# Eight weight combinations moved from a mix of GpSimd and VectorE to VectorE alone, in a fused sliding-window attention and feed-forward kernel

## The chip, the cores and the metric

The kernel runs on one core of one Trainium2 chip. A core has a matrix engine (TensorE, "PE" in the profile; its weight loads are "PEld"), a vector engine (VectorE, "DVE"), an activation engine (ScalarE, "ACT"), a general engine (GpSimd, "POOL") and a synchronization engine (SyncE, "SP") that here only issues transfers. The metric is the device time of one execution in microseconds (us). Before the change it is 304.42 us, the median of three runs (302.83, 304.42 and 305.78).

## What is computed

Attention over 8 batches, 8 heads, 576 positions, 64 numbers per head. Each position attends to the positions at most 32 away:

```
scores = q @ k.T / sqrt(64);  mask = |pos_i - pos_j| <= 32
attn   = softmax(where(mask, scores, -1e9))
x      = (attn @ v), heads side by side          # 4608 tokens x 512
h      = x @ w_in                                # 512 -> 2048
g      = 0.5 * h * (1 + tanh(c * (h + 0.044715 h^3)))
out    = g @ w_out                               # 2048 -> 512
```

## The kernel before

**Tiles.** The 4608 tokens are cut into nine tiles of 512 (`t` = 0 to 8). While tile `t` goes through the feed-forward part, the attention of batch `b = t + 1` is computed in its gaps, as far as there is one. Attention writes the transposed result into `xT`; `ffn_in` (L563) multiplies it with `w_in`, ScalarE applies the gelu (L571), and `ffn_out` (L737) multiplies with `w_out`.

**Fewer products.** The second matrix product of tiles 1 to 8 is done by a scheme of the Strassen-Winograd kind: seven products of half-size blocks in place of eight, after sums of blocks have been made. The sums of gelu's output are made at L680 by VectorE for every tile. In the last two tiles (7 and 8) part of the first product is done in that way too (`in_mixed`, L615). This needs combinations of blocks of `w_in`: for each of two units, A and B, four of them, S1 = A21 + A22, S2 = S1 - A11, S3 = A11 - A21 and S4 = A12 - S2. They are made once, by `in_w` (L590), each one an instruction on 128 x 512 numbers of type fp16, and are kept in SBUF. S2 reads S1, and S4 reads S2; S3 reads `w_in` alone.

**Order.** It is written by hand. Each engine executes its own instructions in the order of the program. The main loop counts steps `i` = 0 to 112 in each tile; a step issues one matmul of `ffn_out`, and a plan says at which step a piece of attention is issued: scores (`s`, L454), the multiplication of the exponentials by the mask (`m`, L476), the sums and the weighting by v (`v`, L481 and L491), and the normalizing of a group (`x`, L526, or L532 for a batch's tail). The second group's normalizing, `x1`, stands at step 50; the tail's mask, `m4`, stands at step 84. Behind each product of `ffn_out` VectorE takes the result out of PSUM or adds it up (L748, L750, L752, L757, L760, L766, L775).

**GpSimd's queue.** Near the start of each tile, GpSimd waits for a transfer (the copy `after`, L952) and issues five loads of v for the next batch (L194 four times, then L198). Its next work in tiles 3 and 4 is the pair of combinations for unit B; then come the tile's stores (L699, L697), which wait for the last sums of the tile. GpSimd doesn't take part in the steps: a combination that is issued at step 92 runs on it as soon as the queue ahead is empty and its inputs are there.

Of the kernel before, what the change touches and what calls it, by code (L numbers as in the profile page):

```python
# [78 lines left out]
def kernel(  # L79
# [9 lines left out]
    nc = tc.nc  # L89
    B, H, S, D = q.shape  # L90
# [4 lines left out]
    NT = NTOK // 512  # L95
# [473 lines left out]
    def gelu(t, n):  # L569
        fc = column(t, n)  # L570
        nc.scalar.activation(gTs[t][:, fc, :], phs[fc], AF.Gelu_apprx_tanh)  # L571
        if t and n % 4 == 3:
            sums(t, n // 4)
# [3 lines left out]
    def in_w(eng, unit, *which):  # L577

        i = UNITS[unit]
        A11, A12, A21, A22 = (w_in16[:, d:d + 2, c + 256 * i:c + 256 * i + 256] for c in (0, 1024) for d in (0, 2))  # L580
        if (unit, "s") not in mixed:
            halves = [(rawp if unit == "A" else yp).tile([128, 2, 2, 256], FP16, name="wc" + unit + str(x),
                                                         tag=("qr", "kr")[x] if unit == "A" else "yo") for x in range(2)]
            mixed[unit, "s"] = [half[:, x] for half in halves for x in range(2)]
        S1, S2, S3, S4 = mixed[unit, "s"]
        mixed[unit, "w"] = dict(A11=A11, A12=A12, A22=A22, S1=S1, S2=S2, S3=S3, S4=S4)
        for x in which:
            dst, a, b, op = ((S1, A21, A22, ALU.add), (S2, S1, A11, ALU.subtract),
                             (S3, A11, A21, ALU.subtract), (S4, A12, S2, ALU.subtract))[x - 1]
            eng.tensor_tensor(dst, a, b, op=op)  # L590
# [77 lines left out]
    def combine(i, eng):  # L668
        dst, x, y = wino["todo"][i]
        eng.tensor_tensor(dst, x, y, op=ALU.subtract)  # L670
# [240 lines left out]
    for t in range(NT):  # L911
        b = t + 1
        att = b < B
        if t:
            for fc in range(begun):
                ffn_in(t, fc, 3, 4, then=False)
            for fc in range(begun):
                gelu(t, fc)
            if att and b > 1:
                parts = cast_and_turn(b)  # L920
            if t >= NT - 2:
                if t == NT - 2:
                    in_x(t)
                in_mixed(t)
            for fc in range(begun, NF if t < NT - 2 else 0):
                ffn_in(t, fc)
                if t == 1 and fc == 3:
                    parts[0]()
                    combine(4, nc.vector)
                if t == 1 and 6 <= fc < 10:  # L930
                    cast_v(2, fc - 6)
                if t == 1 and 9 <= fc < 14:
                    parts[1](fc - 9)
                if t == 1 and fc == 8:
                    trans_tails(1, psO.tile([128, 8, 128], FP16, name="pt", tag="O"))
                if t == 2 and fc == 10:
                    parts()
                if t > 1 and fc == 8 and att:
                    pair_v(b, nc.vector.tensor_copy)
        plan = PLAN_0 if not t else PLAN_1 if t == 1 else PLAN if att else {40: "v-1", 66: "x-1"} if t == B - 1 else {}  # L940

        def group(g):
            return (b, g) if g >= 0 else (b - 1, 4)

        if plan and t:
            load_table(exp_set)
        if t and b + 1 < B:
            load_qk(b + 1)
        ods = {}
        for i in range(113 if t else 65):  # L950
            if t and i == (4 if t > 1 else 46) and b + 1 < B:
                nc.gpsimd.tensor_copy(after, KLs[b % 2][:, 3, 0:1])  # L952
                load_v(b + 1)
                if t == 1:
                    load_tails(3, nc.gpsimd)
            for act in plan.get(i, "").split():
                kind, at = act[0], int(act[act.index("@") + 1:]) if "@" in act else None
                g = int(act[1:].split("@")[0])
                if kind == "w":
                    if g == 3:  # L960
                        cast_w(wo[g], w_out16[:, 12:16, :], cs=(0, 1), on_dve=(0,))
                    else:
                        cast_w(wo[g % 3], w_out16[:, 4 * (g % 3):4 * (g % 3) + 4, :], on_act=(1, 3),
                               cs={1: range(4), 2: (0, 1), 5: (2, 3)}[g])
                elif kind == "e":
                    cast_vt(1) if g == 4 else cast_v(1, g)
                elif kind == "k":
                    cast_early(1, g, (nc.vector, nc.vector))
                    if g == 2:
                        cast_tails(0, nc.gpsimd, even)  # L970
                elif kind == "t":
                    trans_tails(0, spare(at)[0], even)
                elif kind == "r":
                    trans_pair(1, g, *spare(at), copy=nc.scalar.copy if g == 2 else nc.vector.tensor_copy)
                elif kind in "np":
                    pair = psS.tile([128, 2, 512], FP32, name="ps_od", tag=f"S{at}")
                    for x in range(2):
                        if kind == "n":
                            sum_up(1, g + x, pair[:, x, :], groups[(1, g + x)])
                        else:  # L980
                            ods[g + x] = (pair[:, x, :], lts[g + x])
                            times(1, g + x, pair[:, x, :], groups.pop((1, g + x)))
                    if kind == "n":
                        n = size(1, g)
                        lts[g], lts[g + 1] = lt4[:, g, :], lt4[:, g + 1, :]
                        for x in range(2):
                            nc.scalar.activation(lts[g + x][:, 0:n], pair[:, x, 0:n], AF.Ln)
                        for x in range(2):
                            nc.scalar.activation(lts[g + x][:, 0:n], lts[g + x][:, 0:n], AF.Exp, scale=-1.0)
                elif kind == "u":  # L990
                    cast_w(wo[g], w_out16[:, 12:16, :], on_act=(3,), cs=(2, 3))
                    cast_tails(1, nc.gpsimd)
                    load_qk(2)
                elif kind == "c":
                    if g == 1:
                        B12 = combine_w()
                    combine(g, nc.vector)
                elif kind == "s":
                    score(*group(g), at)
                    if t == 1 and g == 4:  # L1000
                        load_table(gelu_set)
                elif kind == "d":
                    pair_chunk(b, g, nc.vector.tensor_copy)
                elif kind == "m":
                    mask(*group(g))
                elif kind == "v":
                    bb, gg = group(g)
                    o, d = weigh(bb, gg, at)
                    ods[g] = (o, invert(bb, gg, d))
                    if t and g < 0 and b + 1 < B:  # L1010
                        load_vt(b + 1)
                    if t > 1 and g == (3 if att else -1):
                        load_table(gelu_set)
                else:
                    spread(*group(g), *ods[g])
            if t == NT - 2 and i == 84:
                in_x(t + 1)
            if t in (3, 4) and i == 92:
                in_w(nc.gpsimd, "B", *((1, 2) if t == 3 else (3, 4)))
            if t == NT - 3 and i in (86, 90):  # L1020
                in_w(*((nc.vector, "A", 1, 2) if i == 86 else (nc.gpsimd, "A", 3, 4)))
            if t == 2 and i in (40, 44):
                store(0, *later[1 if i == 40 else 3])
            if t == 1 and i == 30:
                cast_vt(2)
                store(0, *later[0])
                store(0, *later[2])
            if t == 1 and i in PAIR_1:
                pair_v(2, nc.vector.tensor_copy, PAIR_1[i])
            if t == 0 and i < 64:  # L1030
                ffn_out_0(*ORDER_0[i])
            elif t and i < 112:
                ffn_out(t, i)
        if t == 0:
            wino_rest(B12)
            load_table(gelu_set)
        else:
            ffn_last(t)
        begun = 3 if t < NT - 1 else 0
        for fc in range(begun):  # L1040
            ffn_in(t + 1, fc, 0, 3)
# [28 lines left out]
```

## Time and profile before

The page gives the profiled execution by its span alone; of the three times, the one that lies nearest to this span is 305.78 us.

| | |
|---|---|
| times of the three runs | 302.83, 304.42, 305.78 us |
| span of the profiled execution | 305.7 us |
| PE busy | 288.9 us (95%) |
| DVE busy | 214.1 us (70%) |
| ACT busy | 195.7 us (64%) |
| POOL busy | 99.7 us (33%) |
| mean granted TensorE clock | 0.992 |
| L590 on POOL | 6 instructions, 1.16 to 1.61 us each |
| L590 on DVE | 2 instructions, 0.42 us each |

A row of the timeline has the start in us, the duration in us, the engine, the line, the operation, what it writes and reads, its shape, and in brackets how long its engine was idle before it and what ended this. Rows that follow each other on one engine with the same line are merged, with their number behind an x. The rows of the chain of waits have start, duration and the engine or transfer that the end of the program can be traced back to. The rows of the window table have the window, its length, busy time and number of instructions for PE, PEld, DVE, ACT and POOL, then the granted TensorE clock as a share of full speed, the DMA share and GB/s.

### The profile page before, as it was taken

Reading aid. Unit: us, or ns where it says so; the run is one execution under the profiler, and the core shown is the slowest. Engines: PE = TensorE matmul, PEld = TensorE weight load, DVE = VectorE, ACT = ScalarE, POOL = GpSimd, SP = SyncE. Lnnn points to the kernel's source line nnn. Section 1 sums busy time; section 2 is a strip of 40 time slices with the busy share of each in tenths; the row PEclk is TensorE's granted clock in tenths of the full one; section 3 lists DMA queues with packets and bytes.
Section 4 is the critical chain, followed back from the end, with each engine's and each line's share of the span. In section 5 each row is a group of like instructions: output and inputs, shape, how many; then the busy total and the mean of one; then the engine's idle time right before and its main releaser. Section 6 shows DMA issues by size and latency. Waiting matters only on the chain.

```text
span 305.7 us, 7286 instructions
## 1 busy us (share of the span) xinstructions
PE 288.9 (95%) x2941; PEld 184.7 (60%) x2941; DVE 214.1 (70%) x467; ACT 195.7 (64%) x313; POOL 99.7 (33%) x149
## 2 busy tenths in 40 slices
PE   7879999899899899999999799999999999999994
PEld 2434444445674388448844586468646867786683
DVE  4562577789876866958685948866896678865672
ACT  5865767669576776579657844787578755725700
POOL 3425515301574070607180905141540060006000
PEclk9999999999999999999999989999999999999999
DMA  7999999999699999899987993989694022004013
GB/s 220 203 303 385 368 282 250 226 154 223 174 225 202 171 243 215 162 147 219 168 189 121 239 145 84 145 205 182 114 188 65 2 54 88 2 0 136 3 38 102
DMA packets 115944, 50.76 MB, mean 166 GB/s; under 512 B 97495, under 2 KB 109399, under 8 KB 115910
## 3 DMA queue, kind: packets, MB, share of 16 engines
q1 hardware_dynamic: 86756, 37.62, 58.7%
q0 software_dynamic: 28032, 11.62, 25.8%
q10 hardware_dynamic: 1122, 1.06, 1.1%
q8 instruction: 23, 0.38, 0.6%
q14 instruction: 11, 0.09, 0.1%
HBM read 36.70 MB, written 9.44 MB: 151 GB/s over the span
## 4 chain that ended last, share of the span: by engine, by line
PE 57%; DMA 20%; SPq 10%; ACT 6%; DVE 4%; issue 1%; POOL 0%; DVEq 0%
PE mm L737 26%; PE mm L563 11%; PE ph L563 10%; SPq L182 5%; DMA wst<-in_moe_w_in_dram 5%; DMA tr<-in_q_dram 3%; DMA kr<-in_k_dram 3%; DMA KT<-k 3%; DMA wst<-in_moe_w_out_dram 2%; PE ps_s L454 2%; SPq L240 2%; PE pu L615 2%; DVE s L680 2%; PE ps_d L481 2%; ACT gT L639 2%; DMA tr<-in_k_dram 2%
## 5 line engine op out<-in xcount | busy, mean ns | idle before, releaser
L563 PEld LDWEIGHTS <-w_in 128*128 128x128 f16 x512 | 49.6, 98 | 58.8 <-DVE w_in L228 1.0
L563 PE MATMUL ph<-xT,w_in 128*128 128x512 f16 x256 | 64.1, 379 | 1.2 <-DVE w_in L228 0.5
L563 PE MATMUL mm<-xT,w_in 128*128 128x512 f16 x256 | 63.9, 379 | 0.1
L571 ACT ACTIVATE gT<-mm 128x512 f16<-128x512 f32 x60 | 35.6, 597 | 33.3 <-PE mm L563 32.7
L737 PEld LDWEIGHTS <-s 128*128 128x128 f16 x512 | 49.4, 98 | 7.6 <-issue 0.9
L699 POOL DMA_DIRECT2D out_dram<-y x55 | 32.5, 599 | 60.1 <-DVE y L766 45.9
L737 PE MATMUL mm<-t,s 128*128 128x256 f16 x376 | 45.1, 273 | 0.6 <-DVE y L750 0.2
L737 PEld LDWEIGHTS <-gT 128*128 128x128 f16 x384 | 36.5, 99 | 8.0 <-issue 0.7
L467 ACT ACTIVATE pe<-ps_s 128x960 f16<-128x960 f32 (+1 forms) x31 | 29.6, 976 | 17.7 <-PE ps_s L454 17.5
L571 ACT ACTIVATE gT<-ph 128x512 f16<-128x512 f32 x58 | 32.2, 599 | 10.7 <-PE ph L563 10.7
L680 DVE TENSOR_TENSOR s<-gT 128x512 f16<-128x512 f16 x64 | 26.8, 419 | 15.0 <-ACT gT L571 14.0
L737 PE MATMUL mm<-w_out,gT 128*128 128x256 f16 x256 | 34.3, 280 | 0.1
L104 ACT ACT_TABLE_LOAD x18 | 23.1, 1283 | 2.2 <-issue 1.9
L516 ACT ACTIVATE lt<-ps_d 128x480 f32<-128x480 f32 (+2 forms) x28 | 15.6, 556 | 12.1 <-PE ps_d L481 8.4
L517 ACT ACTIVATE lt<-lt 128x480 f32<-128x480 f32 (+3 forms) x36 | 21.1, 586 | 1.1
L476 DVE TENSOR_TENSOR pe<-pe,band 128x960 f16<-128x960 f16 x28 | 21.0, 765 | 0.9 <-ACT pe L467 0.9
L491 PEld LDWEIGHTS <-V 128*64 128x64 f16 x520 | 14.1, 112 | 7.2 <-DVE V L204 2.8
L194 POOL DMA_DIRECT2D V<-in_v_dram x20 | 17.9, 910 | 1.1 <-issue 0.7
L737 PE MATMUL mm<-t,gT 128*128 128x256 f16 x128 | 16.3, 273 | 0.0
L680 DVE TENSOR_TENSOR s<-s,gT 128x512 f16<-128x512 f16 x32 | 15.3, 478 | 1.1
L454 PE MATMUL ps_s<-QT,KT 64*64 64x128 f16 (+3 forms) x576 | 13.5, 216 | 2.3 <-DMA KT<-k 1.5
L454 PEld LDWEIGHTS <-KT 64*64 64x64 f16 x576 | 9.9, 106 | 8.6 <-issue 3.8
(148 smaller groups left out, 398.4 us busy)
## 6 DMA issues: line engine op xcount, KB each, us to landing
kr<-in_k_dram SPq DMA_DIRECT2D x31, 256.0 KB, 10.9
qr<-in_q_dram SPq DMA_DIRECT2D x6, 1024.0 KB
wst<-in_moe_w_in_dram SPq DMA_DIRECT2D x7, 512.0 KB, 9.3
V<-in_v_dram POOLq DMA_DIRECT2D x20, 128.0 KB, 8.6
wst<-in_moe_w_out_dram SPq DMA_DIRECT2D x2, 1024.0 KB
wst<-in_moe_w_out_dram SPq DMA_DIRECT2D x4, 512.0 KB
qr<-in_q_dram SPq DMA_DIRECT2D x7, 256.0 KB, 8.6
out_dram<-y POOLq DMA_DIRECT2D x6, 192.0 KB, 5.9
```

Of the source, the lines that this page charges most:

```text
L104: nc.scalar.add_instruction(mybir.InstLoadActFuncSet(name=nc.get_next_instruction_name(), act_func_set_id=which, ins=[], outs=[]))
L194: nc.gpsimd.dma_start(V[:, c, :, :], v[b, :, 128 * c:128 * c + 128, :].rearrange("h p d -> p h d"))
L454: nc.tensor.matmul(sides[h][64 * half:64 * half + 64, 4 * n * r:4 * n * r + 4 * n].rearrange("k (j p) -> k j p", j=4)[:, :, p0 - q0:p1 - q ...
L467: nc.scalar.activation(pe, ps[:, :, 0:w], AF.Exp, scale=SCALE)
L476: nc.vector.tensor_tensor(pe, pe, m.rearrange("k (o j) p -> k o j p", o=1).broadcast_to(list(pe.shape)), op=ALU.mult)
L516: nc.scalar.activation(lt[:, 0:n], d[:, 0:n], AF.Ln)
L517: nc.scalar.activation(lt[:, 0:n], lt[:, 0:n], AF.Exp, scale=-1.0)
L563: nc.tensor.matmul(ph, w_in16[:, dc, fc * 128:fc * 128 + 128], xT[:, dc, t * 512 % RING:t * 512 % RING + 512], start=(dc == 0), stop=(dc = ...
L571: nc.scalar.activation(gTs[t][:, fc, :], phs[fc], AF.Gelu_apprx_tanh)
L680: nc.vector.tensor_tensor(dst, x, y, op=op)
L699: eng.dma_start(out_v[b, j, q0 + p:q0 + p + e, cols], yo[m:m + e, cols])
L737: nc.tensor.matmul(pys["apart"][:, 0:256] if apart else py[:, blk, :], lhsT, wino[w][:, f, :], start=(new and i % (8 if one else 16) == 0) ...
```

## The change

All eight combinations are made by VectorE. In tiles 3 and 4 the two of unit B are issued at step 52, behind the second group's normalizing, in place of step 92 on GpSimd. In tile 6 the first two of unit A are issued at step 52 too, in place of step 86, and the last two at step 86, behind the tail's mask, in place of step 90 on GpSimd. Nothing else differs: the instructions of PE, ACT and SP keep their order, VectorE has six more and GpSimd six fewer.

```diff
-            if t in (3, 4) and i == 92:
-                in_w(nc.gpsimd, "B", *((1, 2) if t == 3 else (3, 4)))
-            if t == NT - 3 and i in (86, 90):
-                in_w(*((nc.vector, "A", 1, 2) if i == 86 else (nc.gpsimd, "A", 3, 4)))
+            if t in (3, 4) and i == 52:
+                in_w(nc.vector, "B", *((1, 2) if t == 3 else (3, 4)))
+            if t == NT - 3 and i in (52, 86):
+                in_w(nc.vector, "A", *((1, 2) if i == 52 else (3, 4)))
```

## The prediction

> **What bounds the kernel now.** I read the busy times first: PE is busy for 288.9 of 305.7 us, so time is lost or won only where PE waits or runs slowly. Next I read the chain of waits, and in it the starts of the tiles' first matmuls of `ffn_in` (start, duration, what):
>
> ```profile
> 122.97 0.65 PE mm L563 x3
> ...
> 153.38 0.65 PE mm L563 x3
> ...
> 187.51 0.65 PE mm L563 x3
> ...
> 217.93 0.65 PE mm L563 x3
> ...
> 248.35 0.65 PE mm L563 x3
> ```
>
> These open tiles 3, 4, 5, 6 and 7. Their distances are 30.41, 34.13, 30.42 and 30.42 us. Three tiles agree to 0.01; tile 4 is 3.72 longer with the same work. This is what I have to explain, since one of the three places of the change lies in it. The timeline of DVE, POOL and PE there:
>
> ```profile
> 170.70 1.54 DVE L476 TENSOR_TENSOR pe<-pe,band 128x960 f16<-128x960 f16 x1
> ...
> 172.16 2.30 DVE L476 TENSOR_TENSOR pe<-pe,band 128x960 f16<-128x960 f16 x1
> ...
> 172.03 0.72 POOL L198 DMA_DIRECT2D V<-in_v_dram  x1
> 172.74 1.20 POOL L590 TENSOR_TENSOR wcB<-w_in 128x512 f16<-128x512 f16 x1
> 173.86 1.61 POOL L590 TENSOR_TENSOR wcB<-w_in,wcB 128x512 f16<-128x512 f16 x1
> ...
> 174.52 0.39 PE L481 MATMUL ps_d<-pe,ones 128*64 128x480 f16 x2 [1.60 <-DVE pe L476]
> ```
>
> The reader is to see two masks on VectorE, which take 0.65 each in tile 5 (1.22 for the merged two), here 1.54 and 2.30. The second one ends at 174.46. That is 0.52 after GpSimd's first combination ends (172.74 + 1.20 = 173.94), about one mask's own duration, and GpSimd's second combination is stretched to 1.61 from 1.16 in tile 3. So mask and combination took turns. PE waited 1.60 for this mask. The window table then shows the clock:
>
> ```profile
> 173.00:174.00 1.00, 0.00 (x0) 0.00 (x0) 1.00 (x1) 0.97 (x3) 1.00 (x2) 1.00 2.34 161
> 174.00:175.00 1.00, 0.41 (x4) 0.13 (x4) 1.00 (x3) 0.36 (x1) 1.00 (x1) 0.89 1.62 182
> 175.00:176.00 1.00, 1.00 (x17) 0.81 (x18) 1.00 (x2) 0.95 (x2) 0.47 (x1) 0.50 1.74 181
> ```
>
> Right behind the idle stretch the granted clock falls to 0.50, and it stays there through the window 177 to 178. PE's next 29 matmuls of L737 start at 175.53, against 142.74 + 30.41 = 173.15 if tile 4 had followed tile 3's rhythm: 2.38 are lost by waiting. The other 3.72 - 2.38 = 1.34 are lost at half clock: these 29 take 4.56 in the chain, 3.27 in tile 3.
>
> **What the change removes.** Six combinations leave GpSimd: 1.31 + 1.16 (tile 3), 1.20 + 1.61 (tile 4), 1.17 + 1.16 (tile 6), 7.61 us of an engine that is 33% busy. Its own time is worth nothing; what counts is whom these six held up.
>
> - Tile 3: the third mask took 1.16 in place of 0.65 beside L198 and the first combination. The tile lasted 30.41, so PE had cover for 0.51. Gain 0.
> - Tile 6: an L680 sum took 1.71 beside the first combination of A, against 0.42 for its kind. The tile lasted 30.42, so this too was covered: the product that reads these sums comes later. Gain 0. The tile's stores, now behind S4 at 247.91, can start when L766 ends at 247.33. Nothing waits for them, since the stores of tiles 7 and 8 end the program. Gain 0.
> - Tile 4: the case above. The first mask's extra 0.89 (1.54 - 0.65) was over before any combination ran, so the change doesn't remove it. The second mask then starts at 172.16 as before and, with no combination beside it, takes 0.65, to 172.81. L532 follows (0.56, it overlaps the mask's end by 0.08), to 173.29, and releases the bank for PE's L491 0.04 later, at 173.33. In tile 3's rhythm that is due at 142.42 + 30.41 = 172.83. So 0.50 of the 2.38 stays. PE idles about 0.4 in place of 1.6. Gaps of up to 1.53 elsewhere (PE idle until 107.06, for a transfer) passed with the clock at 1.00, so I take the 1.34 as gone. Gain 3.72 - 0.50 = 3.2.
>
> **What it adds.** Six instructions on VectorE, 0.88 for two (245.85 to 246.73, the pair it already makes in tile 6). At step 52 the pair stands between the second normalizing and L757, which waits for PE:
>
> ```profile
> 240.16 0.65 DVE L526 TENSOR_TENSOR xT<-ps_o,lt 128x480 f16<-128x480 f32 x1
> 242.47 0.69 DVE L757 TENSOR_TENSOR y<-mm,y 128x512 f32<-128x512 f32 x1 [1.66 <-PE mm L737]
> ...
> 245.85 0.42 DVE L590 TENSOR_TENSOR wcA<-w_in 128x512 f16<-128x512 f16 x1
> ```
>
> This idle stretch is 1.66 in tile 6, 1.66 in tile 3 (L757 at 147.51), and 1.59 in the disturbed tile 4 (181.57). It hides 0.88 with at least 0.71 to spare: cost 0. If the cover were gone, L757, the next mask and PE's sums behind it would come up to 0.88 late, per place. The second pair of tile 6 takes exactly the place that S1 and S2 have now, ahead of L766: cost 0. The new waits are S2 on S1, on the same engine (0.04 between the two rows at 245.85), and the buffers: the tiles that unit B takes over were free when GpSimd wrote them at 143.74, and the slot is at about 145.9. Unit A's buffers were free at 223.69; the slot is at 240.8. GpSimd doesn't read SBUF beside any of the slots: in tile 3 its v loads are issued by 143.76 and its next row is at 152.66. A combination beside nothing on GpSimd bounds the cost from below at 0; from above by 0.88 x 3 = 2.6 if all cover were lost.
>
> [...]
> [...]
>
> **The sum.** 305.7 - 3.2 + 0 = **302.5** in the profiled execution's own time, 305.7 by its span. The median of the three runs is 1.3 below that, 304.42, and the range of the three is 2.95, about the size of tile 4's loss: I read 302.83 as a run with little of the disturbance, and 304.42 as one with the wait but without the half clock (305.7 - 1.34 = 304.4). The three times alone don't prove that. So I take 302.5 for the median of after too, 0.6% below the median of before. A run of after with no loss in tile 4 gives 305.7 - 3.72 = 302.0.
>
> **Rivals.**
>
> 1. *GpSimd's transfer issues hold the masks, not the combinations.* The first mask of tile 4 was late before any combination had begun, beside L194 and L198; that speaks for it. Against it: in tile 5 two masks beside L194 took 1.22 together. Then mask 2 waits for L198 until 172.75 and ends at 173.40, L532 at 173.88, L491 starts at 173.92, 1.09 late. That is 302.0 + 1.1 = 303.1, or 304.4 if half clock follows.
> 2. *The disturbance is rare.* If the median run of before had little of it, there is nothing to win, and after stays at about 304.4. For it: the lateness starts with an excess of 0.89 that tiles 3 and 5 don't have. Against it: the spread of the three times.
> 3. *VectorE becomes late, and the time is slower than before.* The place is step 52 of tiles 3, 4 and 6. From the point where VectorE reaches it more than 0.71 late, L757 and the mask behind it are pushed; the price is up to 0.88 per place, and 1.34 if PE's wait then costs it the clock. One such place leaves 302.0 + 2.2 = 304.2; all three 302.0 + 6.7 = 308.7. For it: masks were up to 2.5 late in tile 4. Against it: PE was late with them, and the slot was still 1.59 wide.
> 4. *It doesn't do what it says.* The order of VectorE's program shows the eight combinations where the text puts them, so only their effect is open. I give this no chance of its own.
>
> **How the numbers follow.** Forecast (301.4 to 303.0): 0.60. Rival 1 (303.0 to 304.4): 0.16. Rival 2 (304.0 to 304.8): 0.10. Rival 3 (304.2 to 308.7): 0.08. Below 301.4, for a gain in the first tiles that I don't see: 0.06. A change of about 1% is what a measurement of this kernel can tell from none; the marks are 301.4 and 307.5. Faster: 0.06 and 0.08 of the forecast's lower edge, 0.14. Slower: the upper part of rival 3, 0.05. Within: 0.81. The range reaches from the forecast's lower edge to the end of rival 2, 301.4 to 304.8, which leaves out 0.06 and most of 0.08.
>
> **What would show each step.** Tile 4's distance in the chain: 30.4 to 30.9. Its second mask: 0.65. No granted clock of 0.50 near 175. Pairs of combinations on VectorE at about 145.9, 176.8 and 237.6, 0.88 each, with L757 still waiting for PE behind them. What makes it wrong: masks above 1 us in tile 4 with no combination beside them; a wait of PE at another place; DVE rows of L757 with no idle ahead.

## The result and the profile after

The changed kernel takes 300.99 us, the median of 22 runs (299.28 to 304.40); the kernel before takes 302.97 in 22 runs beside it (300.38 to 307.26). The medians differ by 0.65%; the ratio of the compared runs is 0.9954, with a 95% interval of 0.9931 to 0.9976. Forecast was 302.5 against 304.42, a ratio of 0.9937, inside that interval. As a time in microseconds, 300.99 lies 0.4 under the range, because the kernel before itself has a lower median over 22 runs than over the three that were known.

The ratios leave out runs more than 1.5% above the fastest of the same kernel, and since the stall of tile 4 can itself make a run that long, I give the medians of all runs beside them.

The profiled execution of after has a span of 299.5 us and a time of 301.19, so 1.7 us lie around the span. The chain of waits of after shows the tiles' first matmuls (start, duration, what):

```profile
120.20 0.65 PE mm L563 x3
...
150.70 0.65 PE mm L563 x3
...
181.18 0.65 PE mm L563 x3
...
211.59 0.65 PE mm L563 x3
...
242.01 0.65 PE mm L563 x3
```

Tiles 3 to 6 now last 30.50, 30.48, 30.41 and 30.42 us. Tile 4 is 3.65 shorter than in the profile before (34.13). The timeline of VectorE and GpSimd in tile 4 of after:

```profile
168.01 1.22 DVE L476 TENSOR_TENSOR pe<-pe,band 128x960 f16<-128x960 f16 x2
...
165.66 3.60 POOL L194 DMA_DIRECT2D V<-in_v_dram  x4 [0.36 <-PE ps_s L454]
169.23 0.72 POOL L198 DMA_DIRECT2D V<-in_v_dram  x1
```

Both masks take their undisturbed 1.22 together (1.54 and 2.30 before), though the v loads on GpSimd lie beside them as they did. The window table of after, a little behind this place (window, length, busy time with number of instructions for PE, PEld, DVE, ACT and POOL, then clock, DMA share, GB/s):

```profile
173.00:174.00 1.00, 1.00 (x28) 0.74 (x29) 1.00 (x5) 0.00 (x0) 0.00 (x0) 1.00 2.40 155
174.00:175.00 1.00, 1.00 (x48) 0.79 (x37) 0.32 (x1) 0.80 (x1) 0.00 (x0) 1.00 1.71 159
175.00:176.00 1.00, 1.00 (x11) 0.90 (x10) 0.76 (x2) 1.00 (x3) 0.00 (x0) 1.00 1.62 176
```

PE is busy throughout and the clock is at 1.00. The new instructions stand where VectorE used to wait, here in tile 3:

```profile
142.52 0.65 DVE L526 TENSOR_TENSOR xT<-ps_o,lt 128x480 f16<-128x480 f32 x1
143.08 0.42 DVE L590 TENSOR_TENSOR wcB<-w_in 128x512 f16<-128x512 f16 x1
143.53 0.42 DVE L590 TENSOR_TENSOR wcB<-wcB,w_in 128x512 f16<-128x512 f16 x1
144.82 0.69 DVE L757 TENSOR_TENSOR y<-mm,y 128x512 f32<-128x512 f32 x1 [0.87 <-PE mm L737]
```

L757 still waits 0.87 for PE behind the pair; the pair used up part of an idle stretch.

The two spans differ by 6.2 us. Tile 4 gives 3.65 of it. Another 2.77 come before tile 3 (it opens at 122.97 before, at 120.20 after), where the two programs are the same; that part is not the change's. In the eleven profiles (of this section and the next) whose programs are the same up to there, tile 3 opens anywhere between 118.43 and 122.97. The remaining -0.2 lies in tile 3 and behind the start of tile 8.

### The profile page after: what moved, and what is told of

Its sections match the earlier page's. It is cut to its first block, busy times and chain, and to the rows that moved or that the text cites. A ratio compares the mean times of both kernels' runs of the same rounds, so it can differ in the third digit from the quotient of the medians.

```text
span 299.5 us, 7284 instructions
## 1 busy us (share of the span) xinstructions
PE 286.9 (96%) x2941; PEld 184.4 (62%) x2941; DVE 211.5 (71%) x473; ACT 195.3 (65%) x313; POOL 92.5 (31%) x143
## 4 chain that ended last, share of the span: by engine, by line
PE 58%; DMA 21%; SPq 9%; ACT 6%; DVE 3%; issue 1%; POOL 0%; DVEq 0%
PE mm L737 27%; PE mm L563 11%; PE ph L563 10%; DMA wst<-in_moe_w_in_dram 5%; SPq L182 5%; DMA kr<-in_k_dram 4%; DMA tr<-in_q_dram 4%; DMA wst<-in_moe_w_out_dram 3%; DMA KT<-k 2%; PE ps_s L454 2%; PE pu L615 2%; PE ps_d L481 2%; ACT gT L639 2%; DMA kt<-in_k_dram 2%; DMA tr<-in_k_dram 2%; DVE s L680 2%
## 5 line engine op out<-in xcount | busy, mean ns | idle before, releaser
L737 PE MATMUL mm<-w_out,gT 128*128 128x256 f16 x256 | 32.8, 273 | 0.0
L476 DVE TENSOR_TENSOR pe<-pe,band 128x960 f16<-128x960 f16 x28 | 18.3, 670 | 1.2 <-ACT pe L467 1.2
L737 PE MATMUL mm<-w_out,s 128*128 128x256 f16 x120 | 14.4, 273 | 0.0
```

The costliest lines, as they stand in the source:

```text
L476: nc.vector.tensor_tensor(pe, pe, m.rearrange("k (o j) p -> k o j p", o=1).broadcast_to(list(pe.shape)), op=ALU.mult)
L737: nc.tensor.matmul(pys["apart"][:, 0:256] if apart else py[:, blk, :], lhsT, wino[w][:, f, :], start=(new and i % (8 if one else 16) == 0) ...
```

## The experiments

There are twelve runs of eleven kernels (e12 is e2 again), on three chips, each beside the kernel before on its chip. The last column is the ratio to before with its interval. In e4, e5, e6, e8, e9 and e11 a scratch buffer, `junk`, is declared near the top, so their line numbers are one higher: L477 there is L476 here.

| run | what | median | before | ratio |
|---|---|---|---|---|
| e1 | tile 4's pair alone moved | 301.60 | 302.65 | 0.9957 (0.9925-0.9988) |
| e2 | all moved but tile 4's pair | 304.16 | 302.65 | 1.0006 (0.9961-1.0051) |
| e3 | unit B on GpSimd, gated | 301.46 | 302.65 | 0.9973 (0.9942-1.0005) |
| e6 | slot on VectorE filled threefold | 302.03 | 302.65 | 0.9984 (0.9949-1.0018) |
| e4 | extra additions on GpSimd | 304.96 | 302.97 | 1.0071 (1.0036-1.0105) |
| e5 | extra memsets on GpSimd | 300.76 | 302.97 | 0.9957 (0.9924-0.9990) |
| e7 | VectorE at the old steps | 300.72 | 302.97 | 0.9944 (0.9911-0.9978) |
| e8 | idle pair behind v loads, 4 tiles | 300.97 | 302.97 | 0.9952 (0.9917-0.9986) |
| e9 | tile 4's pair later, on GpSimd | 300.43 | 303.56 | 0.9896 (0.9856-0.9936) |
| e10 | tile 4's pair earlier, on GpSimd | 302.45 | 303.56 | 0.9962 (0.9928-0.9996) |
| e11 | idle pair in tile 4 alone | 300.48 | 303.56 | 0.9898 (0.9853-0.9943) |
| e12 | e2 again | 302.55 | 303.56 | 0.9967 (0.9936-0.9999) |

### Which tile: e1 and e2

```diff
 e1, against before:
-            if t in (3, 4) and i == 92:
-                in_w(nc.gpsimd, "B", *((1, 2) if t == 3 else (3, 4)))
+            if t == 3 and i == 92:
+                in_w(nc.gpsimd, "B", 1, 2)
+            if t == 4 and i == 52:
+                in_w(nc.vector, "B", 3, 4)
 e2, against after:
-            if t in (3, 4) and i == 52:
-                in_w(nc.vector, "B", *((1, 2) if t == 3 else (3, 4)))
+            if t == 3 and i == 52:
+                in_w(nc.vector, "B", 1, 2)
+            if t == 4 and i == 92:
+                in_w(nc.gpsimd, "B", 3, 4)
```

> As before, but the pair of unit B in tile 4 (S3, S4) is made by VectorE at step 52; the pair of tile 3 stays on GpSimd at step 92 and unit A as before. Theory (a combination on GpSimd holds a mask in tile 4, and only there it reaches PE): the whole gain of the change, 0.9954 of before, between 0.993 and 0.998; tile 4 lasts 30.4 to 30.9 us. Rival 1 (the transfer issues hold the masks): 1.000, tile 4 still long in some profiles. Rival 2 (the gain comes from tiles 3 and 6, or from all of them alike): 0.997 to 0.999.

> The change without its tile 4: S3 and S4 of unit B stay on GpSimd behind tile 4's v loads, all the rest as after. Theory: 1.000 of before, 0.998 to 1.002; in the profile a mask of tile 4 can be held. Rival 2: 0.996 to 0.998. If the edits of tiles 3 and 6 cost something on VectorE: above 1.002.

As the theory had it: moving tile 4's pair alone gives 0.9957, moving all but that pair gives 1.0006; their medians, on one chip, are 2.6 us apart. On another chip the same kernel as e2 gives 0.9967 (e12, with a median 1.0 below that of before, where e2's is 1.5 above), and e10, which also leaves only tile 4's pair on GpSimd, gives 0.9962, both with 1 just outside the interval. So most of the gain lies in tile 4; whether some 0.3% of it lies in the other places stays open. The profile of e2 repeats that of before. First its timeline of VectorE, GpSimd and PE, then its window table:

```profile
167.82 3.51 DVE L476 TENSOR_TENSOR pe<-pe,band 128x960 f16<-128x960 f16 x2
...
168.90 0.73 POOL L198 DMA_DIRECT2D V<-in_v_dram  x1
169.60 1.21 POOL L590 TENSOR_TENSOR wcB<-w_in 128x512 f16<-128x512 f16 x1
170.72 1.62 POOL L590 TENSOR_TENSOR wcB<-w_in,wcB 128x512 f16<-128x512 f16 x1
...
171.38 0.40 PE L481 MATMUL ps_d<-pe,ones 128*64 128x480 f16 x2 [1.47 <-DVE pe L476]
```

```profile
172.00:173.00 1.00, 1.00 (x19) 0.78 (x16) 1.00 (x3) 0.97 (x2) 0.34 (x1) 0.75 1.81 178
173.00:174.00 1.00, 1.00 (x6) 0.75 (x5) 0.59 (x2) 0.10 (x1) 0.00 (x0) 0.50 2.35 155
```

The two masks take 3.51 together, PE idles 1.47, the clock falls to 0.50, and tile 4 lasts 34.07. In e1 tile 4 lasts 30.49. But e1 also shows what the prediction denied: with the pair of tile 3 on GpSimd, begun early this time (139.90, 19.3 after the tile's first matmul, against 20.9 in the profile before), a mask of tile 3 is held by 0.96 and that tile lasts 31.00 (VectorE, then GpSimd):

```profile
138.12 2.18 DVE L476 TENSOR_TENSOR pe<-pe,band 128x960 f16<-128x960 f16 x2
140.22 0.55 DVE L532 TENSOR_TENSOR xT<-ps_o,lt 128x384 f16<-128x384 f32 x1
...
139.90 1.41 POOL L590 TENSOR_TENSOR wcB<-w_in 128x512 f16<-128x512 f16 x1
```

So tile 3's collision can cost PE too, 0.6 in this execution.

### Engine or place: e3 and e7

```diff
 e3, against after:
             if t in (3, 4) and i == 52:
-                in_w(nc.vector, "B", *((1, 2) if t == 3 else (3, 4)))
+                nc.gpsimd.tensor_copy(after, xT[:, 1, b * S % RING:b * S % RING + 1])
+                in_w(nc.gpsimd, "B", *((1, 2) if t == 3 else (3, 4)))
 e7, against before: nc.gpsimd -> nc.vector in both calls of in_w, steps 92, 86 and 90 kept
```

> As after, but unit B is made by GpSimd, which is made to wait at step 52 for the second group's normalizing (one copy of a 128 x 1 column). So the engine is that of before and the place that of after. Theory (what counts is that no mask is beside it): like after, 0.993 to 0.998 of before; GpSimd's pair lies at about 143 to 146 us in tile 3, and no mask there is longer than 0.7, or only the fourth one, which PE needs 1.6 later. If a combination on GpSimd costs wherever it lies: 1.000.

> The engine of after and the steps of before: the eight combinations on VectorE at steps 92, 86 and 90. Theory (leaving GpSimd is what gains, any slot of VectorE will do): like after, 0.993 to 0.998 of before, tiles 3, 4 and 6 at 30.4 to 30.9. The pairs stand behind the tail's mask in front of L766, where 0.7 us are idle; tile 6 has two pairs there (1.7 us), which can cost it up to 1 us. If the place behind the second normalizing was needed: tiles 3 and 4 are 0.5 to 0.9 longer too.

With GpSimd as the engine, but the pair made to wait for the second normalizing, tiles 3 and 4 last 30.53 and 30.47, and only the fourth mask of tile 3, which PE needs later, is held:

```profile
142.60 1.16 POOL L590 TENSOR_TENSOR wcB<-w_in 128x512 f16<-128x512 f16 x1
143.84 1.16 POOL L590 TENSOR_TENSOR wcB<-wcB,w_in 128x512 f16<-128x512 f16 x1
...
144.60 0.92 DVE L476 TENSOR_TENSOR pe<-pe,band 128x960 f16<-128x960 f16 x1
```

Its median is 301.46, beside 301.60 for e1; its interval just reaches 1. With VectorE at the old steps (e7) the ratio is 0.9944 and the tiles last 30.42, 30.48 and 30.42 (3, 4 and 6); the loss of up to 1 us that I allowed for the two pairs together in tile 6 is not there. So either edit alone takes the stall out of the profile: leaving GpSimd, or leaving the place beside the first masks; for the second, the gain in time is less certain, as e3's interval says. Step 52 on VectorE was no better than the old steps (0.9954 for after, 0.9944 for e7).

### What holds the mask: e4 and e5

```diff
 e4, against after (e5: six times nc.gpsimd.memset(junk, 0.0)):
                 nc.gpsimd.tensor_copy(after, KLs[b % 2][:, 3, 0:1])
+                for _ in range(3 if t > 1 else 0):
+                    nc.gpsimd.tensor_tensor(junk, w_in16[:, 0:2, 0:256], w_in16[:, 2:4, 0:256], op=ALU.add)
                 load_v(b + 1)
```

> As after, with three more additions of two blocks of w_in on GpSimd (128 x 512, fp16, result not used) ahead of the v loads in tiles 2 to 5, about 3.5 us in each, so that they lie beside the first two masks. Theory (an addition on GpSimd that reads SBUF holds a mask until its end, and the two take turns): masks of 1 to 2.4 us in each of the four tiles, the tiles 1.5 to 3.7 us longer each, by whether the clock is halved; 6 to 15 us over after. If the loss of tile 4 came from the transfers: under 1 us.

> As after, with six memsets of 128 x 512 fp16 on GpSimd at the same place of the same tiles, about 3 us in each: GpSimd is as busy as with the additions but reads nothing. If reading is what holds the mask: masks stay at 0.65, the tiles at 30.4 to 30.6 and the time within 0.5 us of after. If any instruction on GpSimd's data path holds it: as with the additions, 6 to 15 us over after.

VectorE and GpSimd in tile 3 of e4, then in tile 4 of e4:

```profile
138.89 2.46 DVE L477 TENSOR_TENSOR pe<-pe,band 128x960 f16<-128x960 f16 x2
...
138.16 4.21 POOL L955 TENSOR_TENSOR junk<-w_in 128x512 f16<-128x512 f16 x3
...
167.84 1.26 DVE L681 TENSOR_TENSOR s<-s,gT 128x512 f16<-128x512 f16 x1
169.02 1.37 DVE L681 TENSOR_TENSOR s<-gT 128x512 f16<-128x512 f16 x1
170.31 1.37 DVE L681 TENSOR_TENSOR s<-gT,s 128x512 f16<-128x512 f16 x1
...
167.48 3.92 POOL L955 TENSOR_TENSOR junk<-w_in 128x512 f16<-128x512 f16 x3
```

And in tile 3 of e5:

```profile
137.20 1.22 DVE L477 TENSOR_TENSOR pe<-pe,band 128x960 f16<-128x960 f16 x2
...
134.88 3.43 POOL L955 MEMSET junk<- 128x512 f16 x6
```

The additions held the masks in tiles 2 and 3 that lay beside them (two in 2.46 in tile 3) and the sums of gelu's output (1.3 each, 0.42 alone) in tiles 4 and 5, where the additions began earlier. These VectorE instructions have two inputs in SBUF; L749 and L533, which read PE's results beside the additions of tile 3, kept 0.69 and 0.55 (0.69 and 0.56 in e5). The memsets held no mask (two in 1.22). The size of the loss I had wrong: tiles 3, 4 and 5 last 31.29, 32.13 and 32.18, some 0.9 to 1.8 more, and the medians of e4 and e5 are 4.2 apart, not 6 to 15. PE's gaps in these tiles were 0.42 to 1.18 and the clock stayed at 1.00.

### Against which mask: e8 to e12

```diff
 e9, against e2:
             if t == 4 and i == 92:
+                for _ in range(4):
+                    nc.gpsimd.memset(junk, 0.0)
                 in_w(nc.gpsimd, "B", 3, 4)
 e10, against e2: the call of in_w in tile 4 stands ahead of load_vt(b + 1)
 e8, against after (e11: "2 if t == 4"):
                         load_vt(b + 1)
+                        for _ in range(2 if t > 1 else 0):
+                            nc.gpsimd.tensor_tensor(junk, w_in16[:, 0:2, 0:256], w_in16[:, 2:4, 0:256], op=ALU.add)
```

> As e2 (only tile 4's pair on GpSimd), with four memsets of 0.52 us ahead of the pair, which hold no mask, so that the pair begins 2.3 later, at about 21.6 after the tile's first matmul in place of 19.3; the three masks that start at 17.5, 18.0 and 20.1 are over by 20.8. Theory (the cost depends on where the pair falls against the first masks): like after, 0.993 to 0.998 of before, median 300.5 to 301.5. If the pair on GpSimd costs in tile 4 wherever it falls: as e2, median about 304.

> As e2, with the pair ahead of the fifth v load (L198), so that it begins 0.7 earlier, at about 18.5 after the tile's first matmul, right on the second mask. Theory: tile 4 is 2 to 4 us longer in nearly every run, median 303.5 to 305. If an L198 between the v loads and the pair is what makes it costly: like after.

> The kernel of e2 again, beside the three others on one chip: median about 304 and tile 4 at about 34 us in the profile, if e2's reading holds.

> As after, with two additions on GpSimd behind the v loads in each of tiles 2 to 5, where before has its pair in tiles 3 and 4 (result not used). Theory: the loss of before per tile, a mean of 1.4 us over tiles 3 and 4 together, comes in four tiles, most often where GpSimd's v loads start early against PE: 1.5 to 6 us over after; in each tile where a mask of 1 us or more is seen, it lies beside the pair or just ahead of it. Rival (only something particular to tile 4 makes it long): only tile 4 is longer, 1.4 over after.

> As after, with two additions on GpSimd behind tile 4's v loads whose result is not used (e8 in tile 4 alone). Theory: as e2, median about 304, tile 4 longer by 0.6 to 3.7. If e8's small loss in tile 4 was no chance, that is, if the kernel's own pair differs from such an addition: like after, median 301.

e9 and e12 differ by the four memsets alone and ran on one chip. The timelines of tile 4, e9 first, then e12:

```profile
167.40 1.22 DVE L477 TENSOR_TENSOR pe<-pe,band 128x960 f16<-128x960 f16 x2
...
169.67 2.34 POOL L1023 MEMSET junk<- 128x512 f16 x4
171.97 1.16 POOL L591 TENSOR_TENSOR wcB<-w_in 128x512 f16<-128x512 f16 x1
```

```profile
167.46 2.18 DVE L476 TENSOR_TENSOR pe<-pe,band 128x960 f16<-128x960 f16 x2
...
169.65 1.21 POOL L590 TENSOR_TENSOR wcB<-w_in 128x512 f16<-128x512 f16 x1
```

Giving GpSimd 2.3 us more work ahead of the pair makes the kernel 2.1 us faster (300.43 against 302.55), with no overlap of the runs: 299.62 to 300.75 against 301.27 and more. This settles that GpSimd's part in the loss is when it adds, not how much. How often each size of the loss comes is open: the profiles of e12 (tile 4 at 31.07) and e10 (31.67) are of the shortest run of each, 301.27 and 300.52; that of e2 (34.07) is of a run of 304.60, near e2's own median.

The other expectations of this group were met in part. e12's median is 302.55, not 304, and tile 4 lasts 31.07 in its profile, not 34: there one mask was held, not two. The start of the pair doesn't explain this: it began 19.7 after the tile's first matmul in e12 and 19.3 in e2, but 19.3 in tile 3 of e1 too, where one mask was held and the loss was 0.6. e10's pair began at 18.5; the second mask was held to 2.08, but PE idled only 0.74, the clock stayed, and the median is e12's: earlier was not worse. e8 and e11 missed: their profiles show masks of 1.61 and 1.56 in tile 4, and that tile at 31.07 and 31.02, yet their medians are those of kernels without a pair on GpSimd (300.97 beside 300.72 for e7; 300.48 beside 300.43 for e9). An addition whose result is not used cost less in most runs than the kernel's own pair at the same place. Why stays open; a profile shows one execution of each.

## Why the prediction was right, and where not

**The cause of tile 4's 3.72: right.** e1, e2 and e9 against e12 show it: mask held by GpSimd's addition and PE waiting; in the two profiles with the longest such waits, the clock then fell. Rival 1, that the v loads hold the masks, falls: over the 14 profiles more than a hundred masks lie beside such a load with no addition within 2 us behind it, and none is longer than 0.66. Rival 2, that the disturbance is rare, falls as well: all six runs of e9 are shorter than all twelve of e12. But by the medians the loss is 2.1 there and 2.6 between e1 and e2, less than 3.72.

**"The first mask's extra 0.89 was over before any combination ran, so the change doesn't remove it": wrong.** It went with the pair. Tile 4 lasts 30.48 in after, and also in e5, e7 and e9, so of the 0.50 that I left in the sum 0.07 stayed, measured against the 30.41 of tile 3 before. In the profiles 13 masks would have ended freely up to 1.4 us ahead of the first addition's row; 8 were held, by 0.13 to 0.96. Beside the same loads with no addition next in GpSimd's queue, as in after, e7 and e9, none was. So an addition that stands next can hold a mask before its own row begins. I read the row's start as the start of the hold, and the rows beside the first mask should have warned me: tile 5 had the same loads and no delay.

**Half clock, taken as gone with the wait: right.** In these tiles it appears in the two profiles with waits of 1.60 and 1.47, not behind waits of up to 1.18. In after, where PE doesn't wait there, the clock is at 1.00 from 170 to 180.

**Gain 0 in tile 3: right for that execution, wrong as a rule.** In e1 it cost 0.6. Tile 6: no run separates it.

**Cost 0 on VectorE: right.** L757 kept 0.87 of idle time in tile 3, where I had 0.78. How much cover there is shows in e6:

```diff
+            if t in (3, 4, NT - 3) and i == 52:
+                for _ in range(4):
+                    nc.vector.tensor_tensor(junk, w_in16[:, 0:2, 0:256], w_in16[:, 2:4, 0:256], op=ALU.add)
```

> As after, with four more instructions of the same kind and size behind the pair at step 52 of tiles 3, 4 and 6 (their result is not used): 6 x 0.42 = 2.5 us in a stretch that is 1.66 idle. Theory of rival 3's price: L757 and the mask behind it 0.9 late in each of the three tiles; the mask is needed by PE 1.6 later, so the cover of the prediction was larger than it said, and the time is that of after, within 0.3 us. As the prediction priced it: up to 0.9 per place, 2.6 us over after, or 6.7 with half clock.

```profile
143.37 1.79 DVE L1025 TENSOR_TENSOR junk<-w_in 128x512 f16<-128x512 f16 x4
145.08 0.68 DVE L758 TENSOR_TENSOR y<-mm,y 128x512 f32<-128x512 f32 x1
145.68 0.65 DVE L477 TENSOR_TENSOR pe<-pe,band 128x960 f16<-128x960 f16 x1
```

L758 no longer waits for PE, and the mask starts at 26.33 after the tile's first matmul, 0.94 later than in after relative to its tile's 25.39. Tiles 3, 4 and 6 last 30.86, 30.60 and 30.60: about 0.7 us in all for an overrun priced at up to 2.6. So rival 3's price was too high; its condition never came up.

**Mask and combination, which of them waits.** Two masks took 2.46 beside e4's additions, which read SBUF, and 1.22 beside e5's memsets, which only write. The order of the rows doesn't tell which one has to wait: the second mask's row in tile 4 of before starts 0.58 ahead of the addition's (172.16 and 172.74), and it took 2.30.

**The sum.** The term that was mis-sized is the base. I took 305.7, the span, for the profiled execution's time; with the 1.7 that after shows around its span it was, by this estimate, about 307.4, as long as the slowest of the 22 runs (307.26). So the profile showed an execution in which two masks were held and the clock fell, and its 3.7 is near the upper end of what tile 4 costs. The forecast for the median, 1.9 less, came out right (2.0 less), because it set the 302.5 against the median and not against the profile; by the right base it would have been 307.4 - 3.2 = 304.2, no gain on the median. Nor does the spread of the three times, 2.95, show what I read into it: the opening of tile 3 alone differs by 4.54 between profiles of programs that are the same up to there. The agreement of the size is thus partly luck; the mechanism and the sign are not.

## What to carry to other kernels

Here a cheap instruction on GpSimd without a wait ran as soon as its queue was empty, not where it stands in the program (at 172.74, as the row of the last v load ended), and such additions held masks, which take 0.65 alone, to up to 2.30 and sums of gelu's output, 0.42 alone, to up to 1.71. Before moving one to another engine, look at what lies beside it: a wait of GpSimd for the right event (e3) or some writes ahead of it (e9) took the stall out of tile 4 as VectorE at the old steps did (e7): 30.47, 30.48 and 30.48. And when several tiles should be alike, take the difference of their lengths first: 30.41, 34.13, 30.42 pointed at the place at once, and at the price in that execution.

## What I had not expected

- A mask can be held before the row of the addition that holds it begins (8 of 13, by up to 0.96 us). What happens in that time no profile here shows.
- PE's waits of 1.60 (before) and 1.47 (e2) in tile 4 were followed by 3.4 us at half clock; the one of 1.53 in before that ended at 107.06 was not. In e2 the clock fell at 172.50, when PE had been busy again for 1.1 us. The length of a wait alone doesn't decide it.
- When GpSimd's queue gets to the pair depends on the tile. The copy L952 that opens it stands 14.3 to 15.0 us behind the first matmul in tile 4 in all 14 profiles, and 14.5 to 17.3 in tile 3; undisturbed, the first two masks start at 17.5 and 18.0. That fits tile 4 being hit, and tile 3 only when L952 was early there (14.5 in e1).
